# Ranking the tokens of a mixture of experts inside the recurrence: one-hot steps per segment, a slot table kept in PSUM, and slot tiles of two sizes

## The chip, the cores and the metric

The kernel runs on one core of one Trainium2 chip. The metric is the device time of one execution in microseconds (us). Most executions agree within about 1%. Some runs fall into a slower state, with a lower granted clock of TensorE in the records; a run is called slow here when it is over 1.5% above the fastest of its kernel. The granted clock is the share of the full TensorE clock that the throttle lets through, 1.00 being full speed. The engines are PE (TensorE), DVE (VectorE), ACT (ScalarE), POOL (GpSimd) and SP (SyncE). In the traces here an instruction that waits holds up those built behind it on its engine; the order in which they are built comes from a scheduler and not line by line from the source (e2 shows it). A **one-hot** is a row of zeros with a single 1, at the place of a number; PSUM is the memory into which PE's matmuls write and add.

## The reference

```python
def _attn_ref(q, k, v, a_re, a_im):          # B, H, S, D = 4, 8, 768, 48
    # a complex decay a is cut to magnitude 0.999, then for each t:
    #   state = a * state + k v^T ;  y[t] = q[t] . Re(state)
...
def _moe_ref(x, modality_id, w_gate, modality_bias, w1, w2):   # x: 3072 x 384, 8 experts
    logits = x @ w_gate + modality_bias[modality_id]
    e_idx = np.argmax(logits, axis=1)
    ...                                       # gate_w: softmax weight of the chosen expert
    for e in range(E):
        mask = e_idx == e
        h = np.maximum(x[mask] @ w1[e], 0.0)
        out[mask] = gate_w[mask, None] * (h @ w2[e])
```

Each token goes to one expert. With the fixed inputs only two of the eight experts are ever chosen, by 1526 and 1546 tokens.

## The kernel before

The recurrence is done in two rounds of 16 **units**, a unit being a segment of 96 time steps of one batch (so one "row tile" of 96 tokens). A unit's matmuls on PE, in their order, are `tk` (transpose of the keys), `wp` (scores), `tz` (transpose of the decayed state), `py` (the sums with V and with the old state), then the logits and the transposed rows:

```python
def front(g, b):
    ...
    nc.gpsimd.memset(V[:, :, D:64], 0.0)          # POOL clears the padding of V and of KT
    nc.gpsimd.memset(KT[:, :, L:], 0.0)
    ...                                            # tk -> KT (ACT copies), wp -> KW (DVE, times mask)
def back(g, b, KW, V, Z):
    if g:
        ...                                        # tz: four transposes of Z
        nc.scalar.copy(Zs[:], zp[:])               # ACT; py waits for Zs
    ...                                            # py: V x KW, then += Zs x QT
    for j in range(J):
        nc.tensor.matmul(lg_ps[...], wgp[:, j, :], yT[:, j, :], ...)     # logits
    for j in range(J):
        nc.tensor.transpose(xp[:, j, :], yTb[:, j, :], identb[:])        # rows of x
    ...                                            # every second unit: tl, sums of the partial logits
```

The second round's elementwise recurrence runs beside the first 16 units; the last 16 units run alone. Then `moe_sorted` ranks all 3072 tokens at once (the **bridge**), all of it behind the last logits:

```python
onlo = ...   # 96 x 32 x 128 one-hot of (slot mod 128): one DVE operation
load = ...   # 96 x 32 x 2 x 38: token number and gate weight on a one-hot of (slot / 128)
for t in range(NT):                                # 32 fp32 matmuls into one PSUM tile
    nc.tensor.matmul(inv_ps, onlo[:, t, :], load[:, t], start=(t == 0), stop=(t == NT - 1))
...          # idg, ids: the token of each slot, for the gathers and the scatters
```

The expert stage then runs 19 tiles of 256 slots. For each: weights of the tile's expert (SP), two gathers of 128 rows (issued by POOL), `h_ps`, `y_ps`, and two scatters of the result (issued by POOL):

```python
nc.gpsimd.indirect_dma_start(out=xg[:], in_=x_rows, in_offset=...(ap=idg[:, c:c + 1], axis=0))
...
nc.gpsimd.indirect_dma_start(out=out, out_offset=...(ap=ids[:, c:c + 1], axis=0), in_=y_sb[:], ...)
```

## Time and profile before

Before: 600.77 us, the median of three runs (597.14 to 602.15). The profiled execution spans 596.2 us.

| stage | from | to | us |
|---|---|---|---|
| first recurrence, then the second beside the first 16 units | 0 | 313.2 | 313.2 |
| last 16 units | 313.2 | 434.3 | 121.1 |
| bridge: last unit's rows to the first h_ps | 434.3 | 477.2 | 42.9 |
| expert tiles | 477.2 | 596.2 | 119.0 |

The next lines come from PE's timeline of one unit (start, length, instruction, and in brackets the idle time before it and what ended it):

```profile
381.27 0.64 PE L216 MATMUL tz<-ident,Z 128*96 128x128 f32 x4
382.64 0.37 PE L232 MATMUL py<-QT,Zs 96*48 96x96 f32 x4 [0.73 <-ACT Zs L218]
384.31 0.36 PE L246 MATMUL lg_ps<-yT,wgp 128*32 128x96 f32 x4 [0.15 <-ACT yT L238]
```

A wait of 0.73 us for Zs and one of 0.15 are all the idle time in this unit of 8.2 us, and the clock of the unit is 1.00.

### The profile page before, as it was taken

What the parts mean: (1) busy time and instruction counts of PE and PEld (TensorE: products, weight loads), DVE (VectorE), ACT (ScalarE), POOL (GpSimd) and SP (SyncE); (2) the same over time, 40 slices, a digit from 0 to 9 for tenths busy, and PEclk for the clock granted to TensorE, in tenths of its full rate; (3) what the DMA queues carried; (4) which work ended last, traced back from release to release, by engine and by line L of the source; (5) the groups of instructions that cost most, each with busy time, mean ns of one, the idle gap of its engine ahead of it and who ended that gap; (6) DMA issues with size and microseconds to landing.
All of it is one profiled execution on the core that took longest, in us unless ns stands there. A gap on an engine that the chain in (4) does not pass through costs nothing. (4 is left out here: it accounts for less than half of the span.)

```text
span 596.2 us, 11093 instructions
## 1 busy us (share of the span) xinstructions
PE 467.6 (78%) x4124; PEld 326.0 (55%) x4124; DVE 356.9 (60%) x859; ACT 273.6 (46%) x615; POOL 105.3 (18%) x168
## 2 busy tenths in 40 slices
PE   3564656464988998999998999999923699999795
PEld 2232323233665665656666777666613677777573
DVE  3987878859699898798631544444366034544342
ACT  5565556446486676676552444444410023333221
POOL 1000101010101110000000000000000276776622
PEclk9677776756699999999996999999965589999999
DMA  6368798999799896445423545344217069999980
GB/s 155 108 161 188 173 201 187 203 194 217 144 229 243 192 213 166 114 118 133 112 92 75 100 104 103 80 101 97 54 8 317 21 239 375 389 348 316 304 275 1
DMA packets 111478, 102.13 MB, mean 171 GB/s; under 512 B 74494, under 2 KB 98658, under 8 KB 111424
## 3 DMA queue, kind: packets, MB, share of 16 engines
q1 hardware_dynamic: 95648, 80.38, 46.3%
q0 software_dynamic: 15776, 21.05, 19.2%
q8 instruction: 32, 0.52, 0.4%
q14 instruction: 22, 0.18, 0.1%
HBM read 97.36 MB, written 31.95 MB: 217 GB/s over the span
## 5 line engine op out<-in xcount | busy, mean ns | idle before, releaser
L228 PE MATMUL py<-KW,V 96*64 96x192 f32 x512 | 80.4, 348 | 0.0
L194 DVE TENSOR_TENSOR KW<-wp,mask 96x384 f32<-96x384 f32 x64 | 35.3, 553 | 68.4 <-PE wp L193 67.1
L148 DVE TENSOR_TENSOR x<-e,an 128x192 f32<-128x192 f32 x192 | 68.0, 354 | 4.3
L481 ACT ACTIVATE hT<-h_ps 128x512 bf16<-128x512 f32 x38 | 22.7, 597 | 92.0 <-PE h_ps L477 92.0
L66 PE MATMUL total<-sqe,ident 128*128 128x384 f32 x48 | 27.4, 660 | 41.8 <-ACT sqe L103 41.8
L193 PE MATMUL wp<-QT,KT 96*64 96x96 f32 x1024 | 57.4, 264 | 2.4 <-ACT KT L187 1.3
L477 PE MATMUL h_ps<-xgT,w1t 128*128 128x256 bf16 x456 | 54.7, 278 | 2.4 <-DMA w1t<-w1b 2.4
L193 PEld LDWEIGHTS wp<-QT,KT 96*64 96x64 f32 x1024 | 50.7, 147 | 6.7 <-ACT KT L187 5.4
L489 PE MATMUL y_ps<-w2t,hT 128*128 128x384 bf16 x304 | 52.5, 326 | 1.9 <-DMA w2t<-w2b 1.9
L477 PEld LDWEIGHTS <-w1t 128*128 128x128 bf16 x456 | 45.3, 100 | 11.1 <-DMA w1t<-w1b 3.6
L155 DVE TENSOR_TENSOR e<-x 128x96 f32<-128x96 f32 x190 | 48.4, 255 | 4.9 <-DMA kh<-e 0.7
L457 POOL DMA_INDIRECT xg<-x_rows,idg x38 | 37.0, 973 | 55.3 <-DVE empty L444 37.2
L186 PE MATMUL tk<-ident,KW 96*96 96x96 f32 x256 | 34.1, 265 | 14.2 <-DMA KW<-kh 9.9
L228 PEld LDWEIGHTS py<-KW,V 96*64 96x64 f32 x512 | 37.1, 142 | 10.6 <-issue 3.9
L496 POOL DMA_INDIRECT out_dram<-y_sb,ids x38 | 37.9, 996 | 26.8 <-ACT y_sb L492 17.3
L232 PE MATMUL py<-QT,Zs 96*48 96x96 f32 x448 | 33.8, 251 | 8.1 <-ACT Zs L218 8.1
L182 POOL MEMSET KT<- 96x256 f32 x32 | 9.9, 311 | 167.5 <-PE wp L193 167.5
L489 PEld LDWEIGHTS <-hT 128*128 128x128 bf16 x304 | 28.9, 98 | 19.4 <-DMA w2t<-w2b 2.2
L116 PE MATMUL tq<-ident,Qh 128*96 128x128 f32 x192 | 27.2, 288 | 14.8 <-DVE Qh L112 14.8
L479 DVE TENSOR_SCALAR hT<-h_ps 128x512 bf16<-128x512 f32 x38 | 26.3, 691 | 18.5 <-PE h_ps L477 17.1
L494 DVE TENSOR_SCALAR y_sb<-y_ps,inv 128x384 f32<-128x384 f32 x19 | 11.7, 618 | 41.6 <-PE y_ps L489 41.6
L116 PEld LDWEIGHTS tq<-ident,Qh 128*96 128x96 f32 x192 | 21.3, 133 | 27.9 <-issue 13.5
(125 smaller groups left out, 820.5 us busy)
## 6 DMA issues: line engine op xcount, KB each, us to landing
w1t<-w1b SPq DMA_DIRECT2D x19, 768.0 KB, 7.8
w2t<-w2b SPq DMA_DIRECT2D x19, 768.0 KB, 7.8
kh<-e SPq DMA_DIRECT2D x24, 384.0 KB, 2.9
KW<-kh SPq DMA_DIRECT2D x32, 288.0 KB, 4.0
w1b<-in_moe_w_dram POOLq DMA_DIRECT2D x8, 768.0 KB, 7.9
w2b<-in_moe_w_dram POOLq DMA_DIRECT2D x8, 768.0 KB, 8.5
cB<-c_scr SPq DMA_DIRECT2D x56, 96.0 KB, 3.7
ab<-in_a_re_dram SPq DMA_DIRECT2D x24, 192.0 KB, 4.2
```

The costliest lines, as they stand in the source:

```text
L116: nc.tensor.transpose(tp[:, i, :], Qh[:, t4 + i].rearrange("p c d -> p (c d)"), ident[:])
L148: nc.vector.tensor_tensor(x[:], E[c][:, i, :, None, :].broadcast_to([P, 2, 2, D]), an[:, i].rearrange("p (u w) d -> p u w d", u=2), Alu.mult)
L155: done = nc.vector.tensor_tensor(to, x[:, 0], x[:, 1], Alu.add)
L186: nc.tensor.transpose(tp[:, i, :], KW[:, h4 + i, 0:C], ident[:L, :L])
L193: nc.tensor.matmul(wp[u * 64:(u + 1) * 64, i, :], KT[:, h4 + i, u * 64:(u + 1) * 64], QT[:, p, :], start=True, stop=True)
L194: nc.vector.tensor_tensor(KW[:, h4:h4 + 4, C:], wp[0:L], mask[:, None, :].broadcast_to([L, 4, L]), Alu.mult)
L228: nc.tensor.matmul(py[u * 64:(u + 1) * 64, i, :], V[:, 2 * j + u, :], KW[:, 2 * j + u, :], start=True, stop=(g == 0))
L232: nc.tensor.matmul(py[u * 64:u * 64 + D, i, C:], Zs[:, j, u * 64:u * 64 + D], QT[:, p, :], start=False, stop=True)
L457: nc.gpsimd.indirect_dma_start(out=xg[:], out_offset=None, in_=x_rows, in_offset=bass.IndirectOffsetOnAxis(ap=idg[:, c:c + 1], axis=0))
L477: nc.tensor.matmul(h_ps[:, f, :], w1t[:, k, ff * 128:(ff + 1) * 128], xgT[:, k, :], start=(k == 0), stop=(k == KD - 1))
L489: nc.tensor.matmul(y_ps[:], hT[:, f, s * 128:(s + 1) * 128], w2t[:, f, :], start=(f == 0), stop=(f == NF - 1))
L496: sc = nc.gpsimd.indirect_dma_start(out=out, out_offset=bass.IndirectOffsetOnAxis(ap=ids[:, c:c + 1], axis=0), in_=y_sb[:], in_offset=None ...
```

## The change

The intent is to take the ranking off the bridge. Each step (`take`) ranks two or four row tiles as soon as their logits are there, builds their one-hots and adds them by matmul into a table of slots that stays in PSUM for the whole round. Logits and x rows come from one fp32 matmul per pair of heads. The slots fall into 12 tiles of 256 and 7 of 128. The gate weight travels with the row, and a tile's indices are copied by POOL from the table's column.

```diff
-                nc.tensor.matmul(lg_ps[...], wgp[:, j, :], yT[:, j, :], ...)
-                nc.tensor.transpose(xp[:, j, :], yTb[:, j, :], identb[:])
...
+            for j in range(J):
+                nc.tensor.matmul(xw[:, j, :], yT[:, j, :], sel[:, j, :], start=True, stop=True)
+            nc.vector.tensor_reduce(lg[:, m, :], xw[:, :, C:]..., op=Alu.add)
...
+        queue = [(m, m + 4) for m in range(0, own, 4)] + [(own + w, own + w + NB) for w in range(0, G * NB, NB)]
+        for w, _ in enumerate(us):
+            if r == NR - 1 and w and queue[0][1] <= own + w + 1:
+                rt.take(*queue.pop(0))
...
+    def take(self, m0, m1):
+        ...                                        # l, mx, sh, cand, best, oneh: small DVE operations
+            nc.tensor.matmul(rank[:, i, :], self.tri[:], oneh[:, i, :], ...)
+            nc.tensor.matmul(rank[:, i, :], self.ones[:], self.acc, ...)
+        ...                                        # own, pos, part: small DVE operations
+        eng = nc.vector if last else nc.gpsimd
+        for i in range(n):
+            onlo = rp.tile([TP, 128], BF16, name="onlo", bufs=3)
+            eng.tensor_scalar(onlo[:], self.io[:, 0:128], part[:, 0, i:i + 1], None, Alu.is_equal)
+            ld = rp.tile([TP, 2, self.NC], BF16, name="ld", bufs=3)
+            eng.tensor_scalar(ld[:, 0], self.io[:, 0:self.NC], part[:, 1, i:i + 1], self.p1[:], Alu.is_equal, Alu.mult)
+            eng.tensor_scalar(ld[:, 1], ..., float(TP * self.tile_of[m0 + i]), Alu.is_equal, Alu.mult)
+            for a in range(2):
+                nc.tensor.matmul(self.table[:], onlo[:], ld[:, a], ...)
...
+        idx = fp.tile([128, 2, 2], U32, name="idx", bufs=6)
+        nc.gpsimd.tensor_copy(idx[:], rt.rows[:, bass.ds(co, 2), :])
```

## The prediction

> **What bounds the kernel now.** I first read the busy time of each engine by stretches, to find the stages and what is full in each. The columns are the stretch, its length, then busy us and instruction count of PE, PEld, DVE, ACT, POOL, the granted clock, the DMA share, GB/s.
>
> ```profile
> 141.00:300.00 159.00, 144.16 (x1441) 98.41 (x1442) 132.13 (x351) 100.91 (x242) 12.13 (x35) 0.94 0.74 169
> 315.00:434.00 119.00, 110.42 (x1395) 82.53 (x1396) 48.79 (x117) 49.70 (x143) 7.69 (x32) 0.96 0.42 86
> 434.00:477.00 43.00, 16.42 (x82) 15.02 (x81) 19.21 (x41) 1.33 (x4) 4.55 (x6) 0.53 0.34 119
> 477.00:545.00 68.00, 68.00 (x550) 51.65 (x550) 30.07 (x47) 21.29 (x36) 48.50 (x50) 0.97 0.94 336
> ```
>
> There are five stages: the first recurrence alone (to 141, untouched by the change), the second recurrence beside the first 16 units (to about 313), the last 16 units alone (to 433), the routing bridge (433 to 477), and the expert tiles (477 to the end). The last 16 units are PE's stage: 120 us, 7.5 us each with their start; DVE is busy 41% of it. In the bridge no engine is full: it is a chain. In the expert stage PE and DMA are both full.
>
> Second view, the timeline of the bridge (start, length, engine, instruction, wait before it):
>
> ```profile
> 437.19 0.26 DVE L357 TENSOR_SCALAR is_m<-mid 96x32 f32<-96x32 int32 x2 [3.22 <-DMA mid<-in_moe_modality_id_dram]
> ...
> 448.12 4.42 DVE L430 TENSOR_TENSOR onlo<-io,lo 96x4096 f32<-96x4096 f32 x1
> ...
> 456.82 13.91 PE L438 MATMUL inv_ps<-load,onlo 96*128 96x76 f32 x64 [14.23 <-DVE load L435]
> ...
> 471.50 1.05 POOL L457 DMA_INDIRECT xg<-x_rows,idg  x1 [37.20 <-DVE empty L444]
> ```
>
> The last unit's py ends at 433.2, call it t0. Then a load's landing (to 437.2), 11 us of small DVE operations, 8.7 us of one-hot tables on DVE, 13.9 us of matmuls at a clock of 0.5, then the gather; the first h_ps starts at 477.2, t0+44.
>
> Third view, the timeline of POOL in the expert stage:
>
> ```profile
> 490.14 1.01 POOL L496 DMA_INDIRECT out_dram<-y_sb,ids  x1 [0.30 <-issue]
> 491.46 0.99 POOL L496 DMA_INDIRECT out_dram<-y_sb,ids  x1 [0.30 <-issue]
> 493.14 0.99 POOL L457 DMA_INDIRECT xg<-x_rows,idg  x1 [0.69 <-PE xg_ps L465]
> 494.43 0.97 POOL L457 DMA_INDIRECT xg<-x_rows,idg  x1 [0.30 <-PE y_ps L489]
> 495.70 1.01 POOL L496 DMA_INDIRECT out_dram<-y_sb,ids  x1 [0.30 <-issue]
> ```
>
> A tile takes 5.56 us (490.14 to 495.70), which is PE's 2.62 + 0.34 + 2.60 in the chain. POOL needs four issues of 1.3 us, 5.2 us, so it is nearly full too. It never waits for a scatter to land; that matters below, because landing is slow there. For scatters issued between 500 and 507:
>
> ```profile
> DMA to landing us min/median/max: 6.7/6.8/6.9
> ```
>
> From 477.2 to the end are 119 us: 19 tiles, about 5 us of waits for weights, and 6 us after the last y.
>
> **What the Trainium skill says.** "DMA: Bandwidth & Descriptors", section "Anatomy of one DMA — SWDGE (gpsimd) path": about 2 us of a DMA are fixed, mostly the receipt of the write. The trace agrees where nothing else moves: the last scatters land in 2.1 us; under load it is 6.8. The same page, "Latency and other measured facts", gives a tensor_load (a register load) a floor of about 600 ns. Between a w2t issue ending at 448.00 and the next w1t issue at 448.53, with such a load in between, the trace has 0.53 us. "GPSIMD Engine Reference", section 3.1: best case about 1.8 cycles per element at 1.2 GHz for ordinary work. The trace has only POOL memsets: 204 ns for 128 and 311 ns for 256 elements, 0.84 ns per element and 0.1 us fixed. I estimate from both 0.3 to 0.5 us for the new POOL operations. "TensorE: Matmul & The Clock Gate", Part 1, halves the clock of an idle PE; the bridge shows 0.53 and h_ps's first tile took 4.37 us, not 2.62.
>
> **The change part by part.**
>
> *Units.* lg_ps, xp, yTb, lgT and tl go; one fp32 matmul per pair of heads (104 columns) with a DVE reduce comes. PE: 8 + 4 + 2 records of about 0.07 us (1.0 us) against 8 of about 0.1 us, even. ACT loses two casts of 0.33 and half of 0.49 us per unit, DVE gains about 0.2. Every second unit loses PE's stall around tl, about 0.5 us. In the second stage, where DVE is busy 83%, this nearly cancels: -1 us.
>
> *Start of the last 16 units.* The built order puts the loads of mid, a store of x_rows and the zero row before KW's load on SP, and the exponentials of the first four ranking steps before the first KT copy on ACT. That copy now starts early:
>
> ```profile
> 316.98 0.85 ACT L187 COPY KT<-tk 96x384 f32<-96x384 f32 x2 [2.93 <-PE tk L186]
> ```
>
> The last mid load issues about 314.3 and lands about 317.2. Five bias operations (1.7 us), two steps side by side to sh (1.0), and 14 plus 5 small operations until the third and fourth sh (3.5; dependent ones run 0.21 us apart in the bridge) put KT at 322.7 and 323.8: +6 us.
>
> *Ranking inside the last 16 units.* A step is 15 to 19 DVE operations of about 0.2 us, 3 to 4 us, of which DVE has room for 4 per unit. PE gains 63 rank and 64 table matmuls of about 0.08 to 0.1 us, 11 us, partly in its waits for Zs. But engines run in order: rank after tz, 7 DVE operations (1.5 us), POOL's three operations per row tile (about 1.2 us, so 2.4 or 4.8 us), table, and only then the next tk and wp. By hand this gives 8 to 9 us for a unit with two row tiles and nearly 10 with four, against 7.3 before, and 6.7 for one without. Added over 13 units that is +23; as the scheduler interleaves and some of my orders are pessimistic, I take +12, between 0 and 25.
>
> *Bridge.* From t0: yT, xw, reduce 1.2 us; ten DVE operations 2.1; about 39 of ranking, places and one-hots 8; table matmuls and three conversions 1.6; three register loads and index copies on POOL 1.9; from first gather to h_ps 5.7 as before (471.5 to 477.2). Sum t0+20.5 against t0+44: -23.5 us. Weights are issued near t0+12, early enough.
>
> *Expert tiles.* I evaluated the reference: only two experts are chosen, 1526 and 1546 tokens. So there are 12 big tiles, one small one with 10 rows, and 6 empty small ones, against 13 full and 6 empty big ones. PE's work falls by 7 × 2.7 us. Weight bytes stay. But idx is now copied per tile on POOL, in 6 buffers, and the scatter reads it. In the built order the copy for tile i+6 stands right behind the gathers in step i and waits for both scatters of tile i to land, with the next scatter behind it. A big tile's period becomes landing of the second scatter + 0.5 (copy, gaps) + 1.3 + 1.3. With the load lightened I estimate a landing of 4.8 us (5.4 to 6.3 was seen at 483 to 490): 7.9 us, not 5.56. First h_ps to that second scatter of tile 0 is 9.5 us, eleven periods 87, then to the end 25: landing 5, the two remaining index copies behind scatters 6, gather 4, the last small tile 4, and 6 as before. Sum 121.6 against 119: +2.6 us.
>
> Total: -1 + 6 + 12 - 23.5 + 2.6 = -3.9, so 597 us.
>
> **Rivals.** (a) POOL does not bind: if scatters land in 3.5 us, the period is 6.6, the big phase loses 14 us, then the weights' 30 MB at about 390 GB/s bind and the sum is near 583. For it: less load than before. Against: gathers sit ahead of the scatter in the same queue. (b) The units hide the ranking: +2 for that part, 587; with (a) 573. For it: DVE's 59% idle. Against: the order in which KW, rank and state stand on DVE. (c) The units stall fully, POOL operations at 0.5 us or more: +25 to 30, 612 to 615. For it: 8 table matmuls per step behind 12 POOL operations. (d) Weight DMA binds the small tiles: 7 × 1.6 MB at 330 GB/s need 34 us; the POOL bound leaves that time, so it is hidden.
>
> **Range and chances.** The period is uncertain by 0.6 us over 11 tiles (7 us), the units by 10, the start by 3, the bridge by 2: together about 13. That gives 576 to 617. Faster than 588.8: 0.33, as the change was surely meant to win and (a) or (b) suffices; within 2%: 0.52; slower: 0.15.
>
> **What would show it.** The first h_ps about 20 us after the last py. POOL waiting about 2 us for scatters before each idx copy, with 7.9 us from tile to tile. KT's first copy in the last 16 units waiting for ex, PE idle there near 10 us. Table matmuls idling for POOL. The prediction is wrong if the big tiles keep under 6.5 us, or the last 16 units take no longer than 120 us, or over 150.

## More of the kernel before

The page cuts the span into 40 slices of 14.9 us. These are its rows of PE's busy share in tenths and of the granted clock in tenths of full speed:

```profile
PE   3564656464988998999998999999923699999795
PEclk9677776756699999999996999999965589999999
```

The last 16 units are slices 22 to 29. The first of them, with the wait for KW at the start of the round, has PE at 8 and a clock of 6; in the other seven both are 9. The bridge, slices 30 to 32, shows 2, 3 and 6 with a clock of 6, 5 and 5.

## The result, and the profile after

The changed kernel takes 714.48 us (median of four runs, 713.08 to 716.28), the kernel before in the same session 599.11 us (four runs). The ratio is 1.192, with a 95% interval of 1.186 to 1.199. A ratio is the mean time of one kernel's fast runs over that of the other's in the same rounds, so it isn't quite the ratio of the medians.

| stage | before | after | difference |
|---|---|---|---|
| up to the last 16 units | 313.2 | 315.6 | +2.4 |
| last 16 units (last logits of the first round to last logits) | 121.1 | 238.5 | +117.4 |
| bridge | 42.9 | 21.1 | -21.8 |
| expert tiles | 119.0 | 139.3 | +20.3 |
| span | 596.2 | 714.5 | +118.3 |

The bridge gave what was predicted. The last 16 units took all of the loss, and the expert stage 20 us more. The slices of the page, now 17.9 us each:

```profile
PE   4555563598989899869676778887988187868754
POOL 1010000010100000010746533413032324545223
PEclk9777776659989989896765555555577678998987
```

In slices 19 to 21 the clock is 6, 7 and 6, and then 5 in eight slices running, in which PE is busy six to nine tenths. A half clock in the middle of the busiest stage is what wasn't there before. The same by stages, in the view of stretches (stretch, length, busy us and instructions of PE, PEld, DVE, ACT and POOL, granted clock, DMA share, GB/s):

```profile
316.00:553.00 237.00, 185.03 (x1416) 135.34 (x1416) 77.19 (x327) 42.90 (x108) 85.70 (x118) 0.58 0.21 45
553.00:575.00 22.00, 4.29 (x27) 2.24 (x26) 8.68 (x54) 1.01 (x3) 6.85 (x12) 0.63 0.55 208
575.00:643.00 68.00, 55.03 (x401) 39.34 (x402) 22.40 (x35) 15.40 (x26) 31.09 (x37) 0.90 0.79 273
```

POOL went from 7.7 us of work in the last 16 units (the prediction's second line) to 85.7, and PE's busy time from 110 to 185 us for nearly the same work, at a clock of 0.58 instead of 0.96. The groups of instructions (count, busy us, mean ns, then the idle time before them and what ended it) name the new work:

```profile
L419 POOL TENSOR_SCALAR ld<-io,part,p 96x194 bf16<-96x194 f32 x30 | 30.6, 1020 | 0.0
L417 POOL TENSOR_SCALAR onlo<-io,part 96x128 bf16<-96x128 f32 x30 | 19.1, 636 | 43.2 <-DVE part L413 40.7 <-PE py L227 1.6
L417 DVE TENSOR_SCALAR onlo<-io,part 96x128 bf16<-96x128 f32 x2 | 0.5, 269 | 0.0
L425 PE MATMUL table<-ld,onlo 96*128 96x194 bf16 x64 | 20.1, 315 | 43.9 <-POOL ld L419 20.4 <-POOL ld L420 18.9 <-DVE ld L419 4.3
```

A one-hot takes 636 ns on POOL and 269 on DVE (the last step uses DVE); the two ld operations take 1020 and 986 ns on POOL. So a row tile costs 2.64 us of POOL, and PE waited 43.9 us ahead of the table matmuls, 39.3 of them for POOL. One unit of the steady part on PE:

```profile
429.03 0.56 PE L227 MATMUL py<-QT,Zs 96*48 96x96 f32 x4 [0.48 <-ACT Zs L214]
...
432.68 0.32 PE L425 MATMUL table<-ld,onlo 96*128 96x194 bf16 x1 [0.58 <-POOL ld L420]
...
434.55 0.32 PE L425 MATMUL table<-ld,onlo 96*128 96x194 bf16 x1 [0.85 <-POOL ld L419]
435.58 0.32 PE L425 MATMUL table<-ld,onlo 96*128 96x194 bf16 x1 [0.71 <-POOL ld L420]
```

This unit takes 15.5 us, but only 2.6 of them are waits (0.48 + 0.58 + 0.85 + 0.71). The rest is the same matmuls at half speed: four py records take 0.56 us here and 0.37 before. So there are two losses, waits for POOL and a clock of 0.50, and the second is the larger one. The stretches say the same of the whole stage: PE's idle time (length less busy time) grew from 8.6 us (119.00 - 110.42) to 52.0 (237.00 - 185.03), its busy time by 75. The experiments have to say whether the first causes the second.

The third view of the prediction, POOL's timeline in the expert stage:

```profile
595.75 0.98 POOL L530 DMA_INDIRECT xg<-x_rows,idx  x1 [0.30 <-PE h_ps L553]
601.01 0.18 POOL L526 COPY idx<-rows 128x4 uint32 x1 [4.27 <-DMA out_dram<-y_sb,idx]
601.79 1.02 POOL L572 DMA_INDIRECT out_dram<-y_sb,idx  x1 [0.60 <-PE xg_ps L539]
603.12 0.98 POOL L530 DMA_INDIRECT xg<-x_rows,idx  x1 [0.31 <-issue]
604.40 1.02 POOL L572 DMA_INDIRECT out_dram<-y_sb,idx  x1 [0.31 <-issue]
```

The index copy waits 4.27 us until an earlier tile's scatter has landed, and the next scatter stands behind it. Over the big tiles the second scatters start from 584.83 to 680.54, eleven periods of 8.70 us; before, the period was 5.56.

### The profile page after: what moved, and what is told of

Its sections match the earlier page's. It is cut to its first block, busy times and chain, and to the rows that moved or that the text cites. A ratio compares the mean times of both kernels' runs of the same rounds, so it can differ in the third digit from the quotient of the medians.

```text
span 714.5 us, 11046 instructions
## 1 busy us (share of the span) xinstructions
PE 526.6 (74%) x3917; PEld 367.5 (51%) x3917; DVE 365.0 (51%) x1082; ACT 251.3 (35%) x523; POOL 175.7 (25%) x268
## 3 DMA queue, kind: packets, MB, share of 16 engines
q0 software_dynamic: 14992, 20.37, 15.3%
## 5 line engine op out<-in xcount | busy, mean ns | idle before, releaser
L223 PE MATMUL py<-KW,V 96*64 96x192 f32 x512 | 93.0, 416 | 0.0
L189 PE MATMUL wp<-QT,KT 96*64 96x96 f32 x1024 | 79.2, 318 | 2.2 <-ACT KT L183 1.8
L189 PEld LDWEIGHTS wp<-QT,KT 96*64 96x64 f32 x1024 | 68.2, 185 | 17.1 <-issue 8.2
L223 PEld LDWEIGHTS py<-KW,V 96*64 96x64 f32 x512 | 43.5, 170 | 21.3 <-issue 17.4
L425 PE MATMUL table<-ld,onlo 96*128 96x194 bf16 x64 | 20.1, 315 | 43.9 <-POOL ld L419 20.4
L553 PE MATMUL h_ps<-xgT,w1t 128*128 128x256 bf16 (+1 forms) x456 | 48.3, 268 | 0.0
L182 PEld LDWEIGHTS tk<-ident,KW 96*96 96x96 f32 x256 | 30.4, 160 | 29.7 <-issue 21.8
L239 PEld LDWEIGHTS xw<-sel,yT 128*96 128x96 f32 x256 | 35.3, 202 | 18.8 <-issue 9.0
L239 PE MATMUL xw<-sel,yT 128*96 128x104 f32 x256 | 43.8, 310 | 0.6 <-ACT yT L233 0.6
L214 ACT COPY Zs<-tz 96x512 f32<-96x512 f32 x28 | 16.3, 582 | 79.0 <-PE tz L212 75.5
L112 PE MATMUL tq<-ident,Qh 128*96 128x128 f32 x192 | 28.3, 295 | 21.3 <-DVE Qh L108 21.3
L539 PE MATMUL xg_ps<-identb,xg 128*128 128x128 bf16 x93 | 11.4, 243 | 42.8 <-DMA xg<-x_rows,idx 42.8
L227 PEld LDWEIGHTS py<-QT,Zs 96*48 96x48 f32 x448 | 31.8, 152 | 21.3 <-ACT Zs L214 11.5
```

Of the source, the lines that this page charges most:

```text
L112: nc.tensor.transpose(tp[:, i, :], Qh[:, t4 + i].rearrange("p c d -> p (c d)"), ident[:])
L182: nc.tensor.transpose(tp[:, i, :], KW[:, h4 + i, 0:C], ident[:L, :L])
L189: nc.tensor.matmul(wp[u * 64:(u + 1) * 64, i, :], KT[:, h4 + i, u * 64:(u + 1) * 64], QT[:, p, :], start=True, stop=True)
L223: nc.tensor.matmul(py[u * 64:(u + 1) * 64, i, :], V[:, 2 * j + u, :], KW[:, 2 * j + u, :], start=True, stop=(g == 0))
L227: nc.tensor.matmul(py[u * 64:u * 64 + D, i, C:], Zs[:, j, u * 64:u * 64 + D], QT[:, p, :], start=False, stop=True)
L239: nc.tensor.matmul(xw[:, j, :], yT[:, j, :], sel[:, j, :], start=True, stop=True)
```

## The experiments

All outputs are right. The kernels of one session, up to four, were compared with 7 runs of the kernel before, whose median was 602.7 us for e1 to e4, 597.0 for e5 to e8, 598.2 for e9, e10 and b1, 600.5 for e11, b2 and e12, and 597.1 for e13. Not all sessions ran on the same chip. The medians in this table are of all runs, slow ones included; the ratios are of fast runs alone. Slow were three of four runs of e5, two of four of e6 and e7, two of five of e10, one of four of e11 and e12; the medians of their fast runs are 622.5 (e6), 595.3 (e7), 610.7 (e10), 594.4 (e11) and 595.8 (e12). The stages are from each run's trace, cut as above.

| run | median us | ratio | last 16 units | bridge | expert |
|---|---|---|---|---|---|
| before | 599.1 | 1 | 121.1 | 42.9 | 119.0 |
| after | 714.5 | 1.192 | 238.5 | 21.1 | 139.3 |
| e1 one-hots on DVE | 629.6 | 1.046 | 149.8 | 21.2 | 135.8 |
| e2 table one step late | 680.2 | 1.131 | 210.2 | 21.4 | 134.4 |
| e3 20 index buffers | 696.9 | 1.153 | 239.8 | 21.2 | 117.1 |
| e4 zeros before table | 688.5 | 1.146 | 211.7 | 24.2 | 137.1 |
| e5 table after all units | 652.4 | (slow) | (slow) 182.7 | 22.8 | 133.7 |
| e6 ranking after all units | 628.1 | 1.044 | (slow) 118.5 | 59.2 | 136.1 |
| e7 = e1 + e3 | 601.2 | 0.998 | 149.8 | 21.3 | 110.1 |
| e8 = e7, steps spread | 673.3 | 1.128 | 225.2 | 25.1 | 106.3 |
| e9 = e8, rank and table later | 564.8 | 0.941 | 121.2 | 21.0 | 107.4 |
| e10 = e8 + zeros before rank | 613.7 | 1.022 | (slow) 241.4 | 25.7 | 107.1 |
| e13 = e10 + zeros at step 1 | 607.9 | 1.014 | 159.5 | 24.8 | 108.7 |
| e11 = e9, one-hots on POOL | 595.1 | 0.995 | 147.7 | 21.6 | 109.3 |
| e12 = e9, 6 index buffers | 596.9 | 0.990 | 120.8 | 21.2 | 138.3 |
| b1 before, Zs copied twice | 604.0 | 1.009 | 130.4 | 42.8 | 117.1 |
| b2 before, Zs three times | 667.6 | 1.115 | 196.4 | 42.2 | 118.2 |

### e1: the one-hots on DVE

```diff
-        eng = nc.vector if last else nc.gpsimd
+        eng = nc.vector
```

> The one-hots of all 32 row tiles on DVE instead of POOL, nothing else. Theory A (PE stands in order behind POOL's 2.64 us per row tile, and the granted clock falls with the stalls): the last 16 units go from 238 us to 125 to 150, the granted clock there from 0.5 to above 0.9, and the whole from 714 to 605 to 630 us. Rival B (the stage is long because of the added matmuls, the longer chain of DVE operations and the new xw path, whoever makes the one-hots): the units stay above 200 us and the whole above 680; DVE gets 29 us more to do, so it could even be slower.

629.63 us. The units took 149.8 us, the upper end of what theory A said, and their mean clock was 0.89. PE's wait ahead of the table fell to 5.5 us. Theory A holds, and rival B falls as the main cause: who makes the one-hots is worth 85 us. But 149.8 is not 121, and after the start the clock still fell once, at 414.5 us, in a unit in which PE waited 0.73 us for Zs and then 1.02 for oneh, the chain of DVE operations that rival B names.

### e2: POOL's one-hots, table matmuls one step later

```diff
-            for a in range(2):
-                nc.tensor.matmul(self.table[:], onlo[:], ld[:, a], ...)
+            made.append((onlo, ld))                # 10 buffers each
+        for i, (onlo, ld) in enumerate(self.held): ...   # the matmuls of the step before
```

> POOL makes the same one-hots at the same times, but the table matmuls of a step are issued one step later, from more buffers, so PE has no POOL operation to wait for. Theory A: PE's idle time before the table matmuls falls from 44 us to under 8, the clock comes back above 0.9, the units to 125 to 150 us and the whole to 605 to 635. If POOL's rate were the limit even then (KT's memsets stand on POOL behind one-hots), the units would be near 170 and the whole near 650. Rival B: no change, above 690.

680.18 us, less gain than any number expected of theory A. The trace shows why: PE still waited 30.7 us ahead of the table matmuls. The scheduler had moved the delayed matmuls forward again, into the unit in which POOL was still making these one-hots. The experiment did not do what it was meant to do and says little about A.

### e3 and e7: 20 index buffers, alone and with e1

```diff
-        idx = fp.tile([128, 2, 2], U32, name="idx", bufs=6)
+        idx = fp.tile([128, 2, 2], U32, name="idx", bufs=20)
```

> idx gets 20 buffers instead of 6, so no index copy waits for a scatter to land. Theory C (the index copy behind the scatters sets the period of the big expert tiles): POOL's wait before idx for out_dram falls from 45 us to near 0, a big tile's period from 8.7 us to 5.6 to 6.5, the expert stage from 139 to 112 to 120 and the whole from 714 to 690 to 697. Rival D (the gathers' landing, scatter traffic or the weights bind anyway): the stage stays above 132 and the whole above 706.

> e1 and e3 together. If the two causes are independent, the gains add: 629.6 minus the 17 us of e3, 612 us, between 606 and 618; still slower than the kernel before (602.7). If the expert stage was faster in e3 for another reason, 625 or more.

e3: 696.87 us, at the upper edge of what was expected. No index copy waits for a scatter any more (44.6 us in all in the changed kernel), the big tiles' period is 6.69 us (second scatters from 590.21 to 663.80), a little above the expected 5.6 to 6.5, and the expert stage is 117.1 us instead of 139.3. Theory C holds. e7, with both edits, takes 601.20 us (592.42 to 606.16; the fast two 592.42 and 598.08), below the expected 606 to 618. Its fast runs are the same as the kernel before (ratio 0.998, 0.991 to 1.005). Its units take e1's 149.8 us. The expert stage gained 25.7 us on e1's instead of 22; the rest of what the profiled run gained lies ahead of the last 16 units, in a part that the edits don't touch and whose end moves between 309 and 320 us in these traces.

### e4: matmuls of zeros while PE waits for POOL

```diff
             for a in range(2):
+                for _ in range(0 if first and a == 0 else 10):
+                    nc.tensor.matmul(self.table[:], self.zeros[:, 0:128], self.zeros[:], start=False, stop=False)
                 nc.tensor.matmul(self.table[:], onlo[:], ld[:, a], ...)
```

> As the changed kernel, but before each table matmul but the first, ten matmuls of zeros into the same table (0.08 us each at full clock, some 50 us of added PE work): PE still waits for the same POOL operations, but isn't idle while it does. If the fall of the granted clock to 0.5 is what stretches the other matmuls and it follows from PE's idle gaps, the clock stays above 0.85 and the units fall from 238 to 160 to 190 us although PE has more to do: 640 to 670 in all. If the stalls themselves are the cost, or the clock falls for another reason, the units are as long or up to 50 us longer: 714 to 765.

688.50 us: PE got 630 matmuls more to do, and the kernel became 26 us faster. It is not as fast as the numbers said for the clock theory, but far from those of its rival. The stretch of three steady units here, and then two of the same kind in the changed kernel, in the view of stretches:

```profile
408.86:444.99 36.13, 32.87 (x397) 26.39 (x396) 16.59 (x69) 8.06 (x20) 19.18 (x25) 1.00 0.27 61
```

```profile
421.59:453.21 31.62, 26.37 (x188) 19.36 (x190) 10.95 (x42) 5.51 (x13) 11.58 (x16) 0.50 0.23 49
```

With the filling a unit takes 12.0 us (36.13 / 3) at a clock of 1.00; without it 15.8 (31.62 / 2) at 0.50. POOL does about the same in both, 6.4 us per unit here and 5.8 there. So the half clock does follow from PE's idle time, and it is worth more than 3.8 us per unit, as the 12.0 hold the filling too. The stage as a whole took 211.7 us, above the expected 160 to 190.

### e5: all table matmuls behind the last unit

```diff
+            self.held.append((onlo, ld))           # 32 buffers each
+        if last:                                   # all 64 table matmuls here
+            ... add_manual_dep(first table matmul, last rank matmul)
```

> In e2 the order that was built had moved the delayed table matmuls forward again, so PE kept waiting for POOL. Here POOL makes the same one-hots at the same places as in the changed kernel, but the first table matmul depends on the last rank matmul, so all 64 stand after the units and PE can't wait for POOL inside them. Theory A: the granted clock stays above 0.9, the last 16 units take 125 to 145 us instead of 238, the bridge grows by 6 to 20 us for the 64 matmuls, and the whole is 615 to 645 us. If POOL's operations themselves were harmful (KT's memsets late behind one-hots, POOL beside DVE on the same memory), the units stay above 170 and the whole above 660.

652.44 us, but three of the four runs were slow and so was the profiled one; the one fast run took 638.24. PE can't wait for POOL's one-hots here, yet this line of its waits (us in total, times, longest) shows another door:

```profile
PE py L223 <- POOL V L175: 8.9, 1, 8.9
```

The memset of V's padding stands behind twelve one-hot operations on POOL, and py waits 8.9 us for it. The units that follow ran at a clock of 0.50 from 365 to 428. The time of the fast run is within A's 615 to 645 us, but the units of the profiled run, 182.7 us, are not within its 125 to 145, and that run is slow, so e5 decides nothing by itself; e11 asks the question again.

### e6: all ranking behind the last unit

```diff
+        li = nc.vector.tensor_tensor(l, self.lg[...], ...)
+        add_manual_dep(li, last lg reduce of the last unit)
```

> All ranking after the last unit (every step's first DVE operation depends on the last logits), one-hots on DVE. It shows the units with nothing of the change but the xw matmuls. If these cost nothing, as predicted, the 16 units take 118 to 126 us including their start (the ex before KT is gone, the mid loads ahead of KW stay), clock 0.95 or more; the bridge then holds all of the ranking, 55 to 80 us, and the whole is 640 to 665. Rival B's part that blames xw: units above 135.

628.05 us (the profiled run is a slow one, 631). The units took 118.5 us at a clock of 0.93, so logits and rows from one matmul cost nothing that shows there, as predicted. The whole was below the expected 640 to 665 (the fast runs took 620.70 and 624.21), since the bridge with all of the ranking took 59 us, near the lower end.

### e8: loads earlier, one step of two row tiles per unit

```diff
-        mb, mid loads in Router.__init__ (ahead of KW's load on SP)
+        mb, mid loads at the start of the kernel; zero row stored from POOL's queue
-        queue = [(m, m + 4) ...] + [(own + w, own + w + NB) ...]
+        queue = one pair of row tiles per unit, depending on that unit's lg   # on top of e7
```

> e7, and the start and the spreading mended: the loads of mid and the bias stand at the start of the kernel instead of ahead of KW's load, the zero row is stored from POOL's queue, and each unit gets one step of two row tiles (depending on that unit's logits), so no exponential stands ahead of the first KT copy. Expected: first KT copy of the last 16 units about 6 us earlier than in the changed kernel (counted from the last lg of the first 16), the units 125 to 137 us in place of e1's 150, the whole 592 to 604, so even with or a little faster than the kernel before. If the start is not the cause of those 6 us and the spreading changes nothing: 610 or more, as e7.

673.27 us. It was meant to be the good version and is 72 us slower than e7. The start was mended as expected: from the last logits of the first round to those of the first unit 12.7 us, against 19.3 in the changed kernel. But the units took 225 us. PE's timeline of one of them (only the lines with a wait) and the stretch of that unit:

```profile
425.48 0.17 PE L418 MATMUL rank<-oneh,tri 96*96 96x8 bf16 x1 [0.95 <-DVE oneh L414]
433.46 0.56 PE L228 MATMUL py<-QT,Zs 96*48 96x96 f32 x4 [0.73 <-ACT Zs L215]
```

```profile
423.74:439.01 15.27, 13.60 (x94) 9.52 (x96) 7.27 (x32) 2.86 (x7) 0.51 (x2) 0.50 0.22 47
```

PE is idle 1.7 us of 15.3. No POOL operation is involved, POOL is busy 0.51 us. And the clock is 0.50 to 0.59 in every unit from 333 to 540 us. So POOL is not the cause as such: waits of this size are enough, whoever makes them. After the start the clock first fell at 336.0 us, just after the first step's wait of 1.07 us for oneh.

### e9: rank and table matmuls where PE waits anyway

```diff
+            mm = nc.tensor.matmul(rank[:, i, :], self.tri[:], oneh[:, i, :], ...)
+            if i == 0:
+                add_manual_dep(mm, last wp matmul of a later unit)
+        ...  the table matmuls of the step before get the same dependency (6 buffers)
```

> e8 was slow although no POOL one-hot is left in it: PE waits 0.95 us per unit for oneh ahead of the rank matmuls, and the granted clock stays at 0.50. Here a step's rank matmuls, and the table matmuls of the step before, depend on the last wp matmul of a later unit, so they stand behind tz, where PE waits for Zs anyway. Theory E (an idle gap of PE near 1 us in each unit brings the granted clock to 0.5 and keeps it there, and that is most of the loss): the longest gap per unit falls under 0.6 us, the clock is 1.0, the last 16 units take 118 to 130 us instead of e8's 225, the whole 565 to 590, faster than the kernel before. Rival (the added matmuls, DVE operations or DMAs in the units are the load that makes the clock fall): the clock stays near 0.5, 650 or more.

564.84 us (558.89 to 566.05), ratio 0.941 (0.933 to 0.949): faster than both kernels, as theory E said. The stretches are all units, one unit, the bridge and the expert tiles:

```profile
312.50:433.70 121.20, 110.29 (x1422) 85.77 (x1423) 102.16 (x474) 42.20 (x113) 7.19 (x28) 1.00 0.43 86
390.24:397.92 7.68, 7.02 (x94) 5.40 (x96) 7.04 (x33) 2.66 (x7) 0.51 (x2) 1.00 0.43 96
433.70:454.70 21.00, 3.69 (x21) 1.53 (x20) 8.65 (x55) 0.69 (x2) 8.42 (x24) 0.59 0.59 221
454.70:562.00 107.30, 90.73 (x788) 67.28 (x788) 37.48 (x61) 29.53 (x50) 55.89 (x57) 0.98 0.88 310
```

Compare the unit with e8's: the same 94 matmul records and the same 7 us of DVE, 7.68 us against 15.27. PE's work takes 7.02 us at a clock of 1.00 and 13.60 at 0.50. The rank and table matmuls now stand between tz and the py that waits for Zs, and that wait falls from 0.73 to 0.22 us in this unit. (The edit also ties a step's first DVE operation to the logits of the unit before, so that oneh is ready in time; the two parts were not tried apart.) All of the ranking inside the units thus costs nothing that can be seen: 121.2 us with it, 121.1 before, 118.5 in e6 without it.

### e10 and e13: e8, with the waits filled by zeros

```diff
+            for k in range(14):
+                mm = nc.tensor.matmul(self.table[:], self.zeros[:, 0:128], self.zeros[:], ...)
         # ahead of each step's rank matmuls; e10 from the second step on, e13 from the first
```

> e8 with 14 matmuls of zeros into the table (0.08 us each at full clock) ahead of each step's rank matmuls, behind the unit's logits: the same waits for oneh, but PE is not idle in them. Theory E: the clock goes back above 0.9, a unit from 15.3 us to 8 to 9.5, the whole from 673 to 575 to 610. Rival: more work for a throttled PE only makes it slower, 673 to 695.

> e10 with the filling matmuls also ahead of the first step's rank matmuls (the first of them opens the table). If the pair of waits of 1.07 and 0.67 us at the first step was what sent e10 into its slow executions, the clock now stays above 0.95 in all units (a unit of 8 to 9.5 us) and all four times lie within 1.5% of each other, 598 to 612 us. If the falls come by chance from the remaining waits of 0.73 us, some executions are still above 630.

e10's five runs took 608.86, 610.70, 613.71, 637.09 and 695.95 us, and the profile is of the last of these, a slow one. It shows what happened in this slow execution; no trace of a fast one was kept. The first step has nothing to fill its wait:

```profile
337.03 0.21 PE L425 MATMUL rank<-oneh,tri 96*96 96x8 bf16 x2 [1.07 <-DVE oneh L416]
344.38 0.56 PE L228 MATMUL py<-QT,Zs 96*48 96x96 f32 x4 [0.67 <-ACT Zs L215]
```

```profile
335.21:349.94 14.73, 12.91 (x95) 9.10 (x97) 7.29 (x33) 2.86 (x7) 0.51 (x2) 0.60 0.31 61
349.94:366.50 16.56, 15.83 (x108) 11.53 (x110) 7.28 (x33) 2.86 (x7) 0.51 (x2) 0.50 0.27 60
```

In that unit the clock falls (0.60 is the mean over it), at 338.2 us, after the wait of 1.07 and before that of 0.67, which therefore can't have caused it. It then stays at 0.50 to the end of the units, although the only wait left is 0.73 us in 16.6. The three fast runs of the very same program are 82 to 87 us shorter. e13 fills the first step too: four runs of 605.48 to 610.33 us, and the clock is 1.00 in each of its last 14 units, with a wait of about 0.7 us for Zs still in nearly all of them. So in these two traces the same wait leaves a full clock full and a half clock half. That the first step's wait is what made e10's runs slow is likely but not shown: with two slow runs of five, four fast ones in a row can be luck (about one time in eight), and e13 ran on another chip. e13's unit, 10.2 us, is longer than I expected; 14 matmuls fill more than the wait.

### b1 and b2: the kernel before, with a longer wait

```diff
                 nc.scalar.copy(Zs[:], zp[:])
+                if r == NR - 1:
+                    nc.scalar.copy(Zs[:], zp[:])      # b1: once more, b2: twice more
```

> The kernel before with one line more: in the last 16 units ACT copies Zs twice, so PE's wait for Zs, 0.73 us in every second unit, becomes about 1.3 us. Nothing of the change is in it. Theory E: the clock falls to 0.5 in many of the last 16 units, which go from 120 us to 170 to 235, the whole from 600 to 650 to 715. Rival (the waits only cost their own length): 14 copies of 0.58 us, at most 8 us, 600 to 612.

> The kernel before with Zs copied three times in the last 16 units: PE's wait for Zs becomes about 1.9 us in every second unit and about 1.1 in the others. If waits of PE of this size bring the clock down whatever they stand beside, it falls to 0.5 and the whole is 650 to 720; if they only cost their length, at most 14 times 1.2 us, 600 to 618.

b1: 603.96 us, as the rival said, and the clock stays at 1.00 from 337 us on, with waits of 0.9 to 1.34 us in every second unit. So theory E, as it was put here, failed: one wait of up to 1.34 us did not bring the clock down. b2, with one more copy of 0.58 us: 667.61 us (665.21 to 672.22). The first long wait, and the stretches of that unit and of the rest:

```profile
343.64 0.37 PE L235 MATMUL py<-QT,Zs 96*48 96x96 f32 x4 [1.90 <-ACT Zs L221]
```

```profile
338.69:348.64 9.95, 8.05 (x93) 5.82 (x91) 3.47 (x8) 4.91 (x13) 0.51 (x2) 0.81 0.54 114
348.64:489.41 140.77, 130.75 (x985) 92.61 (x984) 38.13 (x88) 48.04 (x120) 5.34 (x21) 0.52 0.24 53
```

This is the clearest of all: nothing of the change is in this kernel. Its units had 121 us of work at full clock, an extra wait of 1.2 us was put into 14 of them, at most 17 us, and they took 196.4, 75 more; the whole grew by 67.

### e11: e9, with the one-hots back on POOL

```diff
-        eng = nc.vector
+        eng = nc.vector if last else nc.gpsimd
```

> e9 with the one-hots back on POOL (all but the last step), 5.3 us of POOL per unit of about 7.6. If POOL's slow operations only hurt by making PE wait (theory A), the total is that of e9, 565, or up to 20 us more (V's and KT's memsets stand behind one-hots on POOL), clock above 0.9 in the units. If the operations on POOL themselves slow the units (beside DVE, or by making V late as in e5), the clock falls again and the total is above 620.

595.10 us (three runs of 594 to 596, one slow of 634), between the two expectations. The stretches are the first unit with a step, the next three, and the eight from 390 us on:

```profile
328.75:341.29 12.54, 10.31 (x95) 7.04 (x94) 5.32 (x30) 2.57 (x7) 10.52 (x14) 0.74 0.28 58
341.29:379.92 38.63, 38.63 (x278) 29.43 (x280) 18.26 (x79) 8.48 (x21) 16.17 (x23) 0.50 0.26 54
390.00:452.10 62.10, 56.14 (x736) 43.08 (x738) 48.78 (x205) 21.54 (x56) 48.10 (x63) 1.00 0.42 87
```

From 390 on, POOL is busy 48 of 62 us with one-hots, and a unit takes 7.8 us (62.1 / 8), as in e9. So POOL's slow operations are harmless where PE does not wait for them. In the first unit it does (0.24, 1.34 and 0.65 us ahead of the table), the clock falls (at 334.6 us, after the 1.34), and the next three units take 12.9 us each. These four units are most of the 26 us between e11's units and e9's.

### e12: e9, with 6 index buffers

```diff
-        idx = fp.tile([128, 2, 2], U32, name="idx", bufs=20)
+        idx = fp.tile([128, 2, 2], U32, name="idx", bufs=6)
```

> e9 with 6 index buffers again, as in the changed kernel. Theory C: POOL waits for scatters before the index copies again, a big tile's period goes from about 6 to 8.5 us, the whole from 565 to 580 to 592. If the index copies mattered only in the slower kernel: 564 to 572.

596.93 us; the fast three took 589.32 to 598.09, their median 4 us above the expected range. The expert stage of the profiled run is 138.3 us against e9's 107.4, and POOL waits 44.1 us for scatters before index copies. The index buffers are worth 31 us, where the units are mended.

## Why the prediction was wrong

The prediction was 597 us in a range of 576 to 617. Its steps, one by one:

- **Units in the second stage, -1:** measured +2.4. Not decided: the end of this part moves between 309 and 320 us in these traces.
- **Start of the last 16 units, +6:** the first KT copy came at 323.2, against 316.98 before. Right in size. Of the cause, the loads ahead of KW's count for most: PE waited 6.10 us for KW, and tk started at 321.64 against 316.38 before. The bias and ranking operations, which the prediction summed as the chain that ends last, ended at about the same time and held the KT copy at most about 1 us more. With the loads moved and the first steps spread (e8) the first unit was 6.6 us shorter.
- **Ranking inside the last 16 units, +12, between 0 and 25:** this step failed. The stage grew by 117.4, so this term measured about 111 us. It had part of the mechanism, PE in order behind POOL's one-hots, but one size was wrong and one loss was missing. The size is "0.3 to 0.5 us for the new POOL operations": they took 0.64, 1.02 and 0.99 us, 2.64 per row tile instead of 1.2, and PE waited 39 us for POOL. (Its own sum by hand was +23, which it cut to +12 for the scheduler's interleaving; even the +23 was a fifth of what came.) The loss that was not in the sum at all: PE's waits take the clock with them. The steady two-tile unit shows the shares: 15.5 us, against 7.7 in e9 for the same work; waits are 2.6 instead of 0.5, so about 2.1 of the 7.8 us lost are waits and 5.7 are half clock. The prediction had read a clock of 0.53 in the bridge and used it only for the first tile of h_ps. Rival (c), "the units stall fully, POOL operations at 0.5 us or more", named the right condition and priced it at 25 to 30 us because it left the clock at 1.
- **Bridge, -23.5:** measured -21.8. Right.
- **Expert tiles, +2.6:** measured +20.3. The mechanism was right, as e3 and e12 show by taking it away and putting it back; the size was off. The period was 8.70 us instead of 7.9, which is 9 us over eleven tiles, and from the last big tile's second scatter to the end it took 34.0 us (680.54 to 714.5) instead of 25.

The five measured differences sum to +118.3, which is that of the spans. Of the rivals, (a) "POOL does not bind" fell, since POOL waited for scatters before 13 index copies. (b) "the units hide the ranking" fell for this kernel, but e9 shows it to be possible: 121.2 us with all of the ranking. In (d) the weights were hidden in the changed kernel; in e9 the DMA engines are 88% busy in the expert stage, so there they are near the next bound.

What stays open is the whole rule of the clock, but the traces narrow it. In all 17 of them, the two of the comparison and the 15 of the experiments, the clock's records have only the values 1.0 and 0.5, and change only at the bounds of steps of 3.41 us (a whole number of such steps lies between any two changes). I summed PE's idle time in each step, from the last logits of the first round to the last logits. The clock fell 41 times, each time at the end of a step with at least 1.07 us idle. None of the 377 steps with less was followed by a fall, all 27 with more than 1.42 were, and in between it went both ways, 14 falls to 15. It came back 38 times, each time after a step without any idle time. The longest single wait within a step sorts them less well: there 54 steps lie where it went both ways, against 29. e1 shows why: the wait of 1.02 us for oneh lies within one step at 413 us (1.10 idle in all) and across two at 452 us (0.41 and 0.70), and only the first was followed by a fall. These are the three steps; idle is the length less PE's busy time, the next figure:

```profile
411.10:414.51 3.41, 2.31 (x23) 1.49 (x23) 2.20 (x15) 0.93 (x4) 0.00 (x0) 1.00 0.44 98
448.65:452.06 3.41, 3.01 (x32) 2.06 (x27) 1.41 (x7) 1.13 (x4) 0.20 (x1) 1.00 0.32 64
452.06:455.47 3.41, 2.71 (x39) 2.10 (x38) 2.94 (x19) 1.16 (x3) 0.00 (x0) 1.00 0.19 41
```

The step of b1 with the wait of 1.34 us did not bring a fall, that of e10 with 1.15 did, and that of b2 with the wait of 1.90 did. Why steps between 1.07 and 1.42 differ is not shown, nor is how long the clock takes to come back: 203 steps at half clock without idle time were not followed by a rise, and in e11 it stayed at 0.50 for 38.63 us in which the trace shows PE busy all the time. The ends of matmuls are modelled in the traces and some can be missing, so the limits are rough.

## What to carry to other kernels

When work is moved into the stage that fills PE, price a wait of PE not only by its length but also by what it does to the granted clock: here about 1.7 us of waits in a unit (e8), against 0.5 in e9, went with a unit of 15.3 us instead of 7.7. Put dependent matmuls (rank, table) into a place where PE waits anyway and where their inputs are a whole unit old, and fix that place by a dependency, since a scheduler may move them forward again. Look at what holds a small per-tile buffer that a slow transfer reads, and give it enough copies; 6 instead of 20 cost 22 us of the expert stage in e3's comparison and 31 in e12's.

## What the Trainium skill lacked or had wrong

- "TensorE: Matmul & The Clock Gate", Part 1 and "HAM oscillation — how this bites in real kernels": the rule given there is to have no PE-idle gaps above about 3.4 us, with full speed again after about 3.4 us of sustained work. Here a step of 3.41 us with a wait of 1.07 us (e8, e10), or one with a wait of 1.90 (b2), was followed by a clock of 0.50; the least idle time in a step before a fall was 1.07 us. In e11 it stayed at 0.50 through 38.63 us of PE busy without a break, in the slow run of e10 for about 200 us with one wait of 0.73 us in 16.6. The page does mention a clock seen stuck, at a lower rate, as a caveat. The page puts the cost of the ramp, which it calls run-variable, under 1% of a typical span; that is the ramp at the start of a kernel, and b2, at half clock in most of its last units, took 667.61 us against 600.51, 11% more.
- "GPSIMD Engine Reference", section 3.1: 1.03 to 2.6 cycles per element at 1.2 GHz make an estimate of 0.2 to 0.4 us for 194 elements, plus dispatch. A tensor_scalar of 96x194 fp32 to bf16 took 0.99 and 1.02 us on POOL, one of 96x128 0.64; DVE took 0.30, 0.37 and 0.27 us for the same.
- No page that was read for this has the landing of a scatter as the time for which its index tile is held, as it was in this program: with 6 index buffers POOL waited 44.6 us before its copies, with 20 none.
